# Sums of weight blocks and of X on VectorE, X's sums queued behind the sets, raw weight pieces in three DMAs

## The chip, the core and the metric

The kernel runs on one core of a Trainium2 chip. The metric is the device time of one launch in microseconds (us), the median of several runs. A core has five engines that run their own instruction queues side by side: TensorE (PE in the rows, its weight loads PEld), VectorE (DVE), ScalarE (ACT), GpSimd (POOL) and SyncE (SP, which here only issues DMAs). Each queue is in order: an instruction that waits holds all that stand behind it.

## The reference

Three layers follow each other, all in float32, with 4608 tokens (8 batches of 576) and width 512:

```python
p_packed = softmax(p @ k.T / 8) @ v          # 32 packed queries per head
x = softmax(q @ p_packed.T / 8) @ p_packed   # per head, heads side by side: x is 4608 x 512
h = x @ w_in                                 # 512 -> 2048
x = (h * sigmoid(1.702 * h)) @ w_out         # 2048 -> 512
h = maximum(maximum(x @ w1, x @ w2), x @ w3) # 512 -> 768
out = h @ w_out2                             # 768 -> 512
```

## The kernel before

Each float32 product is made of three TensorE matmuls on high and low parts of both operands (`mm3`, L102 to L104), so every operand is first split: ScalarE casts the high part, another engine subtracts it to get the low part.

The program is one list of steps. Each step has a time in the list (`add(t, fn)`), the steps are sorted by it and written out in that order, and a scheduler then sets each engine's queue from the written order and the data. `tc.issue_after(ins)` adds one more rule: what is written inside stands behind `ins` on the same engine. `latest["dve"]` is the newest VectorE instruction of the main work: the low part of g (L503) while the second layer runs, an instruction of a set (L717) while the third layer runs.

The second layer runs in 256 units: `h_unit` makes a tile of h on TensorE (18 matmuls of a unit with its part of the output), ScalarE and VectorE form t and then g (L495, L496, L501, L503), and `out_unit` multiplies g by w_out two units later. While it runs, from about 640 us of the span, the weights of the third layer are made ready in 18 pieces of 128 partitions. `Piece.load` brings the raw bits of a piece by SP (L580, four DMAs, two raw buffers); `Piece.conv` decodes them with five VectorE and two ScalarE instructions (L554 to L563); `Piece.sums` forms a sum over 128x512 (L588) and four sums and differences over 128x128 (L591 to L594); `split_hi` and `split_lo` (L605, L609) split these, and SP writes them to DRAM (`wsa`, `wss`, L598 and L611). 14 pieces stand in the list beside the second layer, four at the start of the third.

The third layer is Strassen's scheme with seven products instead of eight. X is taken in six blocks of 768 tokens. Of each block four quarters B11, B12, B21, B22 are loaded by SP (`load_x`, L655, 384 KB each), four differences T1 to T4 are formed (`sum_x`, L658, 128x768), and seven of the eight are split (`split_x`, L662 on ScalarE and L663 on VectorE). A block then runs nine sets (`Set`, steps p1, p6, p7, p5, p2, p4, p3, each a product of six matmuls over 384 columns), whose results VectorE adds and maximises out of PSUM (L717), and ends with `out2`, the product with w_out2. A set's weights are fetched from `wsa` and `wss` by GpSimd's queue (`load_set`, L628 and L629) two sets ahead. `x_early` and `x_late` are the steps for X: for block 0 the sums run on GpSimd, for the others on VectorE.

Of the kernel before, what the change touches and what calls it, by code (L numbers as in the profile page):

```python
# [13 lines left out]
ALU = mybir.AluOpType  # L14
# [5 lines left out]
P = 128  # L20
# [18 lines left out]
TP_ = [6.0, 8.5, 5.0]  # L39
# [3 lines left out]
def tile_packed_attention_moe(  # L43
# [13 lines left out]
    nc = tc.nc  # L57
# [19 lines left out]
    def f(t):  # L77
        return t.bitcast(F32)
# [373 lines left out]
    latest = {}  # L452
# [88 lines left out]
    wo2, xs, xv, st = {}, {}, {}, {}  # L541
# [28 lines left out]
    class Piece:  # L570
# [3 lines left out]
        def load(self):  # L574
            p_, x = divmod(self.k, 3)
            self.raw = late["r"].tile([P, 2 * TB], I32, tag="raw", bufs=2, name=f"wraw_{self.n}")
            r = self.raw.rearrange("p (a b) -> p a b", a=4)
            for fc, a, o in ((p_, 0, 0), (p_, 1, 1), (p_ + 3, 1, 2), (p_ + 3, 0, 3)):
                c0 = (2 * a + self.kc) * 2 * P
                nc.sync.dma_start(r[:, o], w123[x, fc][:, c0:c0 + 2 * P])  # L580

        def conv(self):
            self.hl = [c_tile(f"wa{y}_{self.n}") for y in range(2)]
            self.v, self.s = conv_late(self.n, self.raw, *self.hl, TB)

        def sums(self):
            v, s, g = self.v, self.s, nc.gpsimd
            g.tensor_tensor(out=v, in0=f(self.hl[0]), in1=f(self.hl[1]), op=ALU.add)  # L588
            v11, v12, v22, v21 = (v[:, y * P:y * P + P] for y in range(4))
            s1, s2, s3, s4 = (s[:, y * P:y * P + P] for y in range(4))  # L590
            g.tensor_tensor(out=s1, in0=v21, in1=v22, op=ALU.add)  # L591
            g.tensor_tensor(out=s3, in0=v11, in1=v21, op=ALU.subtract)
            g.tensor_tensor(out=s2, in0=s1, in1=v11, op=ALU.subtract)
            g.tensor_tensor(out=s4, in0=v12, in1=s2, op=ALU.subtract)  # L594

        def save_a(self):
            for y in range(2):
# [55 lines left out]
    def load_x(j, n, kh, th):  # L653
        c0 = j * BT + th * HT
        nc.sync.dma_start(xv[n], x2d[:, 2 * kh:2 * kh + 2, c0:c0 + HT])  # L655

    def sum_x(eng, o, a, b):
        eng.tensor_tensor(out=xv[o], in0=xv[a], in1=xv[b], op=ALU.subtract)  # L658

    def split_x(n):  # L660
        hi, lo = xs[n][:, 0], xs[n][:, 1]
        nc.scalar.copy(hi, xv[n])  # L662
        nc.vector.tensor_tensor(out=lo, in0=xv[n], in1=f(hi), op=ALU.subtract)  # L663


    def x_early(j, eng):
        return [
            (0, lambda: load_x(j, "B11", 0, 0)),
            (0.1, lambda: load_x(j, "B12", 0, 1)),
            (0.2, lambda: load_x(j, "B22", 1, 1)),  # L670
            (0.3, lambda: load_x(j, "B21", 1, 0)),
            (5.0, lambda: sum_x(eng, "T1", "B12", "B11")),
            (7.0, lambda: sum_x(eng, "T3", "B22", "B12")),
            (9.0, lambda: sum_x(eng, "T2", "B22", "T1")),
        ]

    def x_late(eng):
        return [
            (0, lambda: split_x("B11")),
            (1.0, lambda: sum_x(eng, "T4", "B21", "T2")),  # L680
            (1.1, lambda: split_x("T2")),
            (2.2, lambda: split_x("T3")),
            (3.3, lambda: split_x("T1")),
            (4.4, lambda: split_x("B21")),
            (5.5, lambda: split_x("T4")),
            (6.6, lambda: split_x("B22")),
        ]

    def f_tile(tag, bufs, name, dt=F32):
# [108 lines left out]
    def add(t, fn, *a):  # L798
        plan.append((t, len(plan), fn, a))

    def conv(t, name, src, store, load=6.0, pool=0, step=0.0):
        raws, it = [], []

        def a():
            raws.append(load_raw(name, src))

        def b_():
            it.append(convert(name, raws[0], pool))
            next(it[0])

        def c_():
            next(it[0])

        def d_():
            store(next(it[0]))

        add(t - load, a)
        add(t, b_)
        add(t + step, c_)
        add(t + 2 * step, d_)  # L820
# [13 lines left out]
    def main():  # L834
# [9 lines left out]
        tn = [0.0] * 300  # L844
# [84 lines left out]
        for idx in range(18):  # L929
            pc = Piece(idx // 2, idx % 2)  # L930
            t = TP + idx * TP_[1] if idx < 14 else TB0 - 10 + (idx - 14) * 10.5
            for dt, fn in (
                (-8 if idx > 1 else -TP_[0] + .2, pc.load), (0, pc.conv), (3, pc.sums), (4, pc.save_a),
                (14 if idx < 14 else 8, pc.split_hi), (16.5 if idx < 14 else 9.5, pc.split_lo),
            ):
                add(max(t + dt, last_at + .2), fn)
        for fc in range(NF2):
# [2 lines left out]
            add(t, conv_wo2, fc)  # L940
        add(tn[240] - .1, open_x)
        add(tn[248] - 4, open_raw, 0)
        for dt, fn in x_early(0, nc.gpsimd):
            add(tn[248] - 3.5 + dt * .7, fn)
        for dt, fn in x_late(nc.gpsimd):
            add(tn[250] + 1.5 * dt, fn)
        add(TB0 - .05, open_ff2)
        DS, DO = 7.3, 24.6
        DB = 9 * DS + DO
# [1 line left out]
        for n in range(9 * NBLK):  # L951
            j, r = divmod(n, 9)
# [9 lines left out]
        for j in range(NBLK):  # L962
            t0 = TB0 + j * DB + 9 * DS
            if j < NBLK - 1:
                if j == 0:
                    add(t0 - 14.1, open_x2)
                for dt, fn in x_early(j + 1, nc.vector):
                    add(t0 - 14 + dt, fn)
                for dt, fn in x_late(nc.vector):
                    add(t0 + 1 + dt * 1.6, fn)  # L970
            for tt in range(3):
                add(t0 + tt * DO / 9, out2, j, tt, [0, 3, 1, 4], True, False)
            for tt in range(3):
                add(t0 + DO / 3 + tt * DO / 18, out2, j, tt, [2, 5], False, True)
            for tt in range(3, 6):
                add(t0 + DO * tt / 6, out2, j, tt, [0, 3, 1, 4, 2, 5], True, True)

    if True:
        main()
        for _, _, fn, a in sorted(plan, key=lambda s: s[:2]):  # L980
            fn(*a)
        late["f"].release()
        late["x"].release()
        spp.release()
# [53 lines left out]
```

## Time and profile before

| | us |
|---|---|
| median of 3 runs | 1418.73 (1418.44 to 1420.18) |
| the profiled execution, its own time | 1418.77 |
| its span from first to last instruction | 1416.9 |
| TensorE busy in the span | 1344.9 (95%) |
| VectorE busy | 989.1 (70%) |
| ScalarE busy | 575.2 (41%) |
| GpSimd busy | 322.6 (23%) |

The busy share of VectorE is a mean over stages that differ: in slices of 35 us it lies between 0.5 and 0.9 or more in the first two layers and between 0.2 and 0.7 in the third. So the profile is read here by stretches of the span, and then by what TensorE waits for in each. [...]

### The profile page before, as it was taken

Reading aid. Unit: us, or ns where it says so; the run is one execution under the profiler, and the core shown is the slowest. Engines: PE = TensorE matmul, PEld = TensorE weight load, DVE = VectorE, ACT = ScalarE, POOL = GpSimd, SP = SyncE. Lnnn points to the kernel's source line nnn. Section 1 sums busy time; section 2 is a strip of 40 time slices with the busy share of each in tenths; the row PEclk is TensorE's granted clock in tenths of the full one; section 3 lists DMA queues with packets and bytes.
Section 4 is the critical chain, followed back from the end, with each engine's and each line's share of the span. In section 5 each row is a group of like instructions: output and inputs, shape, how many; then the busy total and the mean of one; then the engine's idle time right before and its main releaser. Section 6 shows DMA issues by size and latency. Waiting matters only on the chain.

```text
span 1416.9 us, 22472 instructions
## 1 busy us (share of the span) xinstructions
PE 1344.9 (95%) x8450; PEld 1278.2 (90%) x8450; DVE 989.1 (70%) x1850; ACT 575.2 (41%) x1212; POOL 322.6 (23%) x436
## 2 busy tenths in 40 slices
PE   5899789999999999999999899699999999999998
PEld 3688789999999989999888899699989999899997
DVE  6799897887666566759899977564646646466362
ACT  3555555664554555545555552131221311213111
POOL 1110244344331035314344222101101001011000
PEclk8999899999999999999999999899999999999999
DMA  8654313561442224125655539765747747476461
GB/s 310 240 189 150 113 55 108 160 198 42 124 127 77 94 66 131 58 75 190 201 173 173 172 126 299 256 227 174 258 161 248 269 160 250 169 259 216 144 205 45
DMA packets 88524, 237.13 MB, mean 167 GB/s; under 512 B 10848, under 2 KB 40032, under 8 KB 81504
## 3 DMA queue, kind: packets, MB, share of 16 engines
q0 software_dynamic: 24640, 132.66, 27.8%
q1 hardware_dynamic: 63776, 103.05, 21.9%
q8 instruction: 66, 1.08, 0.3%
q14 instruction: 42, 0.34, 0.1%
HBM read 191.89 MB, written 43.78 MB: 166 GB/s over the span
## 4 chain that ended last, share of the span: by engine, by line
PE 75%; DVE 16%; DMA 3%; issue 2%; ACT 2%; POOL 1%; SPq 1%; DVEq 0%; ACTq 0%; POOLq 0%
PE p L102 9%; PE p L103 8%; PE p L104 8%; PE acc L102 7%; PE acc L103 7%; PE acc L104 7%; PE accb L103 3%; PE accb L104 3%; PE accb L102 3%; PE h L102 3%; PE h L104 3%; PE h L103 3%; DVE g L503 2%; DVE t L496 2%; DMA xr<-x2d 1%
## 5 line engine op out<-in xcount | busy, mean ns | idle before, releaser
L102 PE MATMUL acc<-g,wo 128*128 128x288 f32 x1024 | 306.3, 302 | 16.2 <-DVE x L523 5.9
L103 PE MATMUL acc<-g,wo 128*128 128x288 f32 x1024 | 303.8, 297 | 7.6 <-DVE g L503 7.5
L104 PE MATMUL acc<-g,wo 128*128 128x288 f32 x1024 | 303.7, 297 | 0.0
L102 PEld LDWEIGHTS acc<-g,wo 128*128 128x128 f32 x1024 | 194.4, 191 | 22.6 <-issue 6.3
L103 PEld LDWEIGHTS acc<-g,wo 128*128 128x128 f32 x1024 | 195.2, 191 | 12.6 <-DVE g L503 10.2
L104 PEld LDWEIGHTS acc<-g,wo 128*128 128x128 f32 x1024 | 195.2, 191 | 0.7 <-issue 0.3
L503 DVE TENSOR_TENSOR g<-t,g 128x288 fp32r<-128x288 f32 x254 | 142.6, 562 | 44.4 <-ACT g L501 41.2
L501 ACT CAST g<-t 128x288 fp32r<-128x288 f32 x256 | 110.8, 433 | 150.9 <-DVE t L496 149.7
L102 PE MATMUL h<-at,pw 128*128 128x288 f32 x512 | 154.8, 303 | 6.0 <-DVE t L496 4.1
L495 ACT ACTIVATE t<-h 128x288 f32<-128x288 f32 x256 | 104.4, 409 | 123.4 <-PE h L104 120.4
L496 DVE SCALAR_TENSOR_TENSOR t<-t,h 128x288 f32<-128x288 f32 x256 | 114.8, 450 | 55.1 <-ACT t L495 52.6
L103 PE MATMUL h<-at,pw 128*128 128x288 f32 x512 | 152.7, 298 | 0.3 <-POOL at L127 0.3
L104 PE MATMUL h<-at,pw 128*128 128x288 f32 x512 | 152.2, 297 | 0.0
L628 POOL DMA_DIRECT2D wa<-wsa x54 | 28.7, 532 | 426.2 <-PE p L104 413.2
L102 PE MATMUL p<-x_T,ws 128*128 128x384 f32 x324 | 109.3, 337 | 11.4 <-DVE m L717 11.4
L103 PE MATMUL p<-x_T,ws 128*128 128x384 f32 x324 | 109.0, 336 | 0.0
L104 PE MATMUL p<-x_T,ws 128*128 128x384 f32 x324 | 108.8, 336 | 0.0
L717 DVE TENSOR_TENSOR u<-s,p 128x384 f32<-128x384 f32 x54 | 29.9, 554 | 112.7 <-PE p L104 112.7
L102 PEld LDWEIGHTS h<-at,pw 128*128 128x128 f32 x512 | 97.0, 190 | 9.6 <-DVE t L496 6.5
L103 PEld LDWEIGHTS h<-at,pw 128*128 128x128 f32 x512 | 97.1, 190 | 0.7 <-POOL at L127 0.5
L104 PEld LDWEIGHTS h<-at,pw 128*128 128x128 f32 x512 | 97.2, 190 | 0.2
L747 ACT COPY s<-p 128x384 f32<-128x384 f32 x54 | 25.9, 479 | 163.3 <-PE p L104 163.3
(187 smaller groups left out, 3150.6 us busy)
## 6 DMA issues: line engine op xcount, KB each, us to landing
ws<-wss POOLq DMA_DIRECT2D x54, 1024.0 KB, 7.6
wa<-wsa POOLq DMA_DIRECT2D x54, 768.0 KB, 4.6
wi<-wsc POOLq DMA_DIRECT2D x48, 512.0 KB, 4.0
raw_k<-in_k SPq DMA_DIRECT2D x32, 288.0 KB, 3.3
raw_q<-in_q SPq DMA_DIRECT2D x32, 288.0 KB, 2.8
x2d<-x SPq DMA_DIRECT2D x16, 576.0 KB, 3.5
wraw<-in_w SPq DMA_DIRECT2D x72, 128.0 KB, 3.3
wss<-ws SPq DMA_DIRECT2D x36, 256.0 KB, 3.0
```

What stands on the lines that cost most here:

```text
L102: nc.tensor.matmul(o, al, bh, start=start, stop=False, skip_group_check=more)
L103: nc.tensor.matmul(o, ah, bl, start=False, stop=False, skip_group_check=more)
L104: nc.tensor.matmul(o, ah, bh, start=False, stop=stop, skip_group_check=more)
L495: nc.scalar.activation(t, o, AF.Tanh, scale=0.5 * 1.702)
L496: nc.vector.scalar_tensor_tensor(out=t, in0=t, scalar=1.0, in1=o, op0=ALU.add, op1=ALU.mult)
L501: latest["act"] = nc.scalar.copy(g[:, 0], gt[n])
L503: latest["dve"] = eng.tensor_tensor(out=g[:, 1], in0=gt[n], in1=f(g[:, 0]), op=ALU.subtract)
L628: nc.gpsimd.dma_start(a, wsa[n % 9].rearrange("p i h b f -> p (i h b f)"))
L717: latest["dve"] = nc.vector.tensor_tensor(out=o, in0=a, in1=b, op=op)
L747: latest["act"] = nc.scalar.copy(self.s1, self.b1)
```

## The change

`Piece.sums` moves its five instructions from GpSimd to VectorE, behind `latest["dve"]`; the first of them adds the decoded high part before its cast instead of the cast one. `Piece.load` takes three DMAs for the same bytes, one of two quarters and two of one. `sum_x` is always on VectorE and also stands behind `latest["dve"]`. The lists `x_early` and `x_late` become `x_loads` (all four quarters at one time) and `x_steps` (sums and splits mixed), which for blocks 1 to 5 begin in the list 1 us behind t0, the list's time for the end of the nine sets of the block ahead; before, three of the four sums stood 9 to 5 us ahead of t0. The times of the steps of a piece change with that: sums at 4 instead of 3, the split at 6.5 and 9 instead of 14 and 16.5.

```diff
             r = self.raw.rearrange("p (a b) -> p a b", a=4)
-            for fc, a, o in ((p_, 0, 0), (p_, 1, 1), (p_ + 3, 1, 2), (p_ + 3, 0, 3)):
-                c0 = (2 * a + self.kc) * 2 * P
-                nc.sync.dma_start(r[:, o], w123[x, fc][:, c0:c0 + 2 * P])
+            src = [w123[x, y].rearrange("p (a k b) -> p a k b", a=2, k=2)[:, :, self.kc] for y in (p_, p_ + 3)]
+            nc.sync.dma_start(r[:, :2], src[0])
+            for a in range(2):
+                nc.sync.dma_start(r[:, 3 - a], src[1][:, a])
...
         def sums(self):
-            v, s, g = self.v, self.s, nc.gpsimd
-            g.tensor_tensor(out=v, in0=f(self.hl[0]), in1=f(self.hl[1]), op=ALU.add)
+            v, s = self.v, self.s
...
-            g.tensor_tensor(out=s1, in0=v21, in1=v22, op=ALU.add)
-            g.tensor_tensor(out=s3, in0=v11, in1=v21, op=ALU.subtract)
-            g.tensor_tensor(out=s2, in0=s1, in1=v11, op=ALU.subtract)
-            g.tensor_tensor(out=s4, in0=v12, in1=s2, op=ALU.subtract)
+            with tc.issue_after(latest["dve"].ins):
+                nc.vector.tensor_tensor(out=v, in0=v, in1=f(self.hl[1]), op=ALU.add)
+                nc.vector.tensor_tensor(out=s1, in0=v21, in1=v22, op=ALU.add)
+                nc.vector.tensor_tensor(out=s3, in0=v11, in1=v21, op=ALU.subtract)
+                nc.vector.tensor_tensor(out=s2, in0=s1, in1=v11, op=ALU.subtract)
+                nc.vector.tensor_tensor(out=s4, in0=v12, in1=s2, op=ALU.subtract)
...
-    def sum_x(eng, o, a, b):
-        eng.tensor_tensor(out=xv[o], in0=xv[a], in1=xv[b], op=ALU.subtract)
+    def sum_x(o, a, b):
+        with tc.issue_after(latest["dve"].ins):
+            nc.vector.tensor_tensor(out=xv[o], in0=xv[a], in1=xv[b], op=ALU.subtract)
...
+    def x_steps():
         return [
...
+            (0, lambda: sum_x("T1", "B12", "B11")),
+            (0.9, lambda: split_x("B11")),
+            (1.8, lambda: sum_x("T2", "B22", "T1")),
+            (2.7, lambda: sum_x("T4", "B21", "T2")),
+            (3.6, lambda: split_x("T2")),
+            (4.5, lambda: sum_x("T3", "B22", "B12")),
...
-                (-8 if idx > 1 else -TP_[0] + .2, pc.load), (0, pc.conv), (3, pc.sums), (4, pc.save_a),
-                (14 if idx < 14 else 8, pc.split_hi), (16.5 if idx < 14 else 9.5, pc.split_lo),
+                (-8 if idx > 1 else -TP_[0] + .2, pc.load), (0, pc.conv), (4, pc.sums), (5, pc.save_a),
+                (6.5, pc.split_hi), (9, pc.split_lo),
...
-        for dt, fn in x_early(0, nc.gpsimd):
-            add(tn[248] - 3.5 + dt * .7, fn)
-        for dt, fn in x_late(nc.gpsimd):
-            add(tn[250] + 1.5 * dt, fn)
+        add(tn[248] - 3.9, x_loads, 0)
+        for dt, fn in x_steps():
+            add(tn[249] + 2 * dt, fn)
...
-                for dt, fn in x_early(j + 1, nc.vector):
-                    add(t0 - 14 + dt, fn)
-                for dt, fn in x_late(nc.vector):
-                    add(t0 + 1 + dt * 1.6, fn)
+                add(t0 - 14, x_loads, j + 1)
+                for dt, fn in x_steps():
+                    add(t0 + 1 + 1.5 * dt, fn)
```

VectorE's queue in the third layer, before, at the end of set 5 of block 0 (the first number in a name such as t_5 or u3_5 is the set; xr0 to xr5 are the raw X buffers, and L658 forms T1 of block 1):

```order
L717 TENSOR_TENSOR u3_5_10756<-u2_5_10747,p7_5_10749 128x384
L717 TENSOR_TENSOR t_5_3_10765<-u3_5_10756,p5_5_10758 128x384
L658 TENSOR_TENSOR xr4_10890<-xr1_10887,xr0_10886 128x768
L717 TENSOR_TENSOR m_3_3_10627<-t_5_3_10765,m_3_3_10627 128x384
L717 TENSOR_TENSOR m_3_0_10637<-p1_5_10727,m_3_0_10637 128x384
```

The same queue now, at the end of set 8, the last of block 0:

```order
L666 TENSOR_TENSOR x_B22_9750<-xr3_10871,x_B22_9750 128x768
L716 TENSOR_TENSOR g2_8_2_10994<-m_6_2_10841,g2_8_2_10994 128x384
L716 TENSOR_TENSOR g2_8_1_11006<-m_6_1_10849,g2_8_1_11006 128x384
L661 TENSOR_TENSOR xr4_10872<-xr1_10869,xr0_10868 128x768
L661 TENSOR_TENSOR xr5_10873<-xr3_10871,xr4_10872 128x768
L661 TENSOR_TENSOR xr1_10869<-xr3_10871,xr1_10869 128x768
L661 TENSOR_TENSOR xr0_10868<-xr2_10870,xr5_10873 128x768
L666 TENSOR_TENSOR x_T2_9752<-xr5_10873,x_T2_9752 128x768
```

T1 of block 1 moved from the middle of set 5 to behind the last instruction of set 8.

VectorE's queue beside the second layer, now, at the first piece (t_181, g_181 and so on are of the units; wa1_0_0 is the low part of piece 0_0, c0 and c1 its work tiles); before, the five sums were not in this queue:

```order
L563 SCALAR_TENSOR_TENSOR wa1_0_0_7653<-c1_0_0_7655,wraw_0_0_7588 128x512
L503 TENSOR_TENSOR g_181_7686<-t_181_7671,g_181_7686 128x288
L592 TENSOR_TENSOR c0_0_0_7654<-c0_0_0_7654,wa1_0_0_7653 128x512
L496 SCALAR_TENSOR_TENSOR t_182_7700<-t_182_7700,h_182_7693 128x288
L593 TENSOR_TENSOR c1_0_0_7655<-c0_0_0_7654 128x128
L594 TENSOR_TENSOR c1_0_0_7655<-c0_0_0_7654 128x128
L131 TENSOR_TENSOR pw_7_1_7373<-pw_3_3_1_7703,pw_7_1_7373 64x512
L595 TENSOR_TENSOR c1_0_0_7655<-c1_0_0_7655,c0_0_0_7654 128x128
L503 TENSOR_TENSOR g_182_7730<-t_182_7700,g_182_7730 128x288
L596 TENSOR_TENSOR c1_0_0_7655<-c0_0_0_7654,c1_0_0_7655 128x128
```

The five sums (L592 to L596) now lie between the units' t and g, over about one and a half units.

The same queue now, at the last units of the second layer, where X of block 0 is made ready:

```order
L666 TENSOR_TENSOR x_T2_9752<-xr_2_9945,x_T2_9752 128x768
L496 SCALAR_TENSOR_TENSOR t_252_10104<-t_252_10104,h_252_10097 128x288
L503 TENSOR_TENSOR g_252_10123<-t_252_10104,g_252_10123 128x288
L661 TENSOR_TENSOR xr_0_9943<-xr_1_9944,xr_0_9943 128x768
L496 SCALAR_TENSOR_TENSOR t_253_10134<-t_253_10134,h_253_10127 128x288
L523 SCALAR_TENSOR_TENSOR x2_227_9412<-acc_248_0_10046,x2_227_9412 128x288
L523 SCALAR_TENSOR_TENSOR x2_227_9412<-acc_248_1_10050,x2_227_9412 128x288
L666 TENSOR_TENSOR x_T3_9753<-xr_0_9943,x_T3_9753 128x768
L523 SCALAR_TENSOR_TENSOR x2_227_9412<-acc_248_2_10054,x2_227_9412 128x288
```

The four sums and all seven splits of block 0 now stand from g_248 on; before, the four sums were in GpSimd's queue, the first split stood at t_236 and the last between g_250 and t_251.

## Rows read from the trace of the kernel before

**Rows 1.** Stretches of the span: length, busy of PE, PEld, DVE, ACT, POOL; clock, DMA.
```profile
core 0: us, PE busy (x) PEld busy (x) DVE busy (x) ACT busy (x) POOL busy (x), PEclk, DMA share, GB/s
640.00:800.00 160.00, 150.92 (x1078) 144.57 (x1078) 148.23 (x283) 89.81 (x202) 58.41 (x78) 1.00 0.58 192
...
810.77:816.64 5.87, 5.87 (x25) 5.87 (x26) 4.37 (x11) 2.44 (x6) 0.00 (x0) 0.50 0.30 89
...
839.00:859.00 20.00, 20.00 (x153) 20.00 (x152) 13.32 (x30) 8.24 (x18) 1.58 (x3) 1.00 0.43 135
870.00:890.00 20.00, 20.00 (x116) 19.53 (x115) 18.80 (x38) 6.80 (x13) 7.38 (x11) 1.00 1.02 333
903.85:915.24 11.39, 0.00 (x1) 0.00 (x1) 1.95 (x4) 0.49 (x2) 0.00 (x0) 0.71 0.83 312
915.24:919.14 3.90, 3.90 (x13) 3.90 (x13) 3.90 (x8) 1.38 (x4) 0.00 (x0) 0.52 0.00 0
950.00:1400.00 450.00, 450.00 (x2430) 428.85 (x2429) 249.59 (x449) 97.90 (x178) 44.52 (x84) 1.00 0.58 200
```

**Rows 2.** Waits of PE from 800 us on: who, for whom, total us, times, longest.
```profile
PE p L102 <- DVE m L717: 11.4, 1, 11.4
PE acc L102 <- ACT g L501: 5.6, 1, 5.6
```

**Rows 3.** Instructions in order of time at the longer wait: start, us, engine, idle before.
```profile
913.29 0.96 DVE L658 TENSOR_TENSOR xr<-xr,xr 128x768 f32<-128x768 f32 x1 [13.01 <-DMA xr<-x2d]
...
915.24 0.69 PE L102 MATMUL p<-x_T,ws 128*128 128x384 f32 x1 [11.39 <-DVE m L717]
```

**Rows 4.** The same view ahead of the shorter wait.
```profile
804.75 2.56 DVE L663 TENSOR_TENSOR x_B<-xr,x_B 128x768 fp32r<-128x768 f32 x1
...
807.45 1.90 POOL L658 TENSOR_TENSOR xr<-xr,xr 128x768 f32<-128x768 f32 x1 [0.95 <-POOL xr L658]
807.60 2.29 DVE L563 SCALAR_TENSOR_TENSOR wo<-c_o,wraw_o 128x512 fp32r<-128x512 f32 x1
```

**Rows 5.** DVE groups by shape, 640 to 812 us: count, busy us, mean ns.
```profile
L503 DVE TENSOR_TENSOR g<-t,g 128x288 fp32r<-128x288 f32 x61 | 32.8, 537 | 3.6 <-ACT g L501 3.6
...
L558 DVE SCALAR_TENSOR_TENSOR c<-wraw,c 128x512 int32<-128x512 int32 x14 | 11.7, 839 | 0.2 <-ACT c L555 0.2
L557 DVE SCALAR_TENSOR_TENSOR c<-wraw,c 128x512 f32<-128x512 uint16 x14 | 11.4, 814 | 0.1
...
L554 DVE TENSOR_SCALAR c<-wraw 128x512 int32<-128x512 int32 x14 | 9.3, 664 | 4.7 <-DMA wraw<-in_w 4.7
L562 DVE TENSOR_SCALAR wraw<-c 128x512 int32<-128x512 int32 x14 | 9.1, 651 | 0.0
L556 DVE TENSOR_SCALAR c<-wraw 128x512 int32<-128x512 int32 x14 | 8.9, 636 | 0.0
```

**Rows 6.** DVE groups by shape, 779 to 800 us.
```profile
L503 DVE TENSOR_TENSOR g<-t,g 128x288 fp32r<-128x288 f32 x9 | 4.0, 448 | 0.0
...
L558 DVE SCALAR_TENSOR_TENSOR c_o<-wraw_o,c_o 128x512 int32<-128x512 int32 x4 | 2.7, 680 | 0.0
L556 DVE TENSOR_SCALAR c_o<-wraw_o 128x512 int32<-128x512 int32 x4 | 1.7, 418 | 0.0
...
L609 DVE TENSOR_TENSOR ws<-c,ws 128x512 fp32r<-128x512 f32 x2 | 1.4, 678 | 0.0
```

**Rows 7.** POOL and DVE in order of time at one piece's sums.
```profile
680.17 1.32 POOL L588 TENSOR_TENSOR c<-wa,wa 128x512 f32<-128x512 f32 x1 [5.69 <-DVE wa L563]
...
680.31 1.47 DVE L562 TENSOR_SCALAR wraw<-c 128x512 int32<-128x512 int32 x1
```

**Rows 8.** Weights of sets 7 and 8, the transfers: start of issues, and time to landing.
```profile
L629 POOL DMA_DIRECT2D ws<-wss x2: 528/532/537, 895.9 to 903.2; - x2
...
DMA to landing us min/median/max: 10.1/10.9/11.8
```

**Rows 9.** ScalarE's copies out of PSUM after the product p1 of set 8.
```profile
931.87 0.48 ACT L747 COPY s<-p 128x384 f32<-128x384 f32 x1 [8.87 <-PE p L104]
```

More of the change, by code (lines that the diff above doesn't have):

```diff
@@ L663, in split_x, with x_loads @@
         nc.vector.tensor_tensor(out=lo, in0=xv[n], in1=f(hi), op=ALU.subtract)
-    def x_early(j, eng):
+    def x_loads(j):
+        for n, kh, th in (("B11", 0, 0), ("B12", 0, 1), ("B22", 1, 1), ("B21", 1, 0)):
+            load_x(j, n, kh, th)
+    def x_steps():
         return [
[L668 to L686, printed above, removed]
+            (0, lambda: sum_x("T1", "B12", "B11")),
[4 more added lines that the diff above has]
+            (4.5, lambda: sum_x("T3", "B22", "B12")),
+            (5.4, lambda: split_x("T3")),
+            (6.3, lambda: split_x("T1")),
+            (7.2, lambda: split_x("B21")),
+            (8.1, lambda: split_x("T4")),
+            (9.0, lambda: split_x("B22")),
         ]
```

## The prediction

> **What bounds the kernel now.** I read the stretches of the span first [rows 1]. From 950 to 1400 us TensorE is busy for all of 450.00 us at a granted clock of 1.00, and VectorE for 249.59: five of the six blocks of the third layer are bound by TensorE, and nothing on VectorE, GpSimd or SP can shorten them. What can be gained lies ahead of that, where TensorE waits. Of the waits from 800 us on two count, 11.4 and 5.6 us [rows 2]. Between 640 and 800 us TensorE has 150.92 us of work, so it stands for 9.1 us in many short waits, beside a VectorE that is busy for 148.23 of 160 [rows 1].
>
> The longer wait: VectorE sits idle for 13.01 us at 900 to 913 us, in front of an L658, the first sum of X for block 1, until X's load lands [rows 3]. In the middle of block 0's sets this holds the L717 instructions that stand behind it in the queue; they empty the PSUM banks, and TensorE starts again only at 915.24, behind one of them [rows 2, 3]. The load was late, but nobody needed it yet: it was the place in the queue that cost time. [...]
>
> The shorter wait: four sums of X for block 0 run on GpSimd, and beside one of them two VectorE instructions take 2.56 and 2.29 us [rows 4]; the size of the first takes 0.96 [rows 3], that of the second 0.68 [rows 6]. The low part of g comes late, and TensorE waits 5.6 us [rows 2]; then its clock is 0.50 for 5.87 us [rows 1].
>
> **Part 1, X's sums of block 1 behind the sets.** In the new queue L661 stands behind the last g of set 8. The set instructions no longer wait for a transfer; the first instructions that need X are the splits behind set 8's first result. p1 of set 8 ended at 931.87 [rows 9], which without the wait and its clock is 931.87 - 11.39 - 1.87 = 918.6. X landed at 913.29 [rows 3], so it is there with 5.3 us to spare. Gain: 11.39, and 3.90 x (1 - 0.52) = 1.87 for the clock, together 13.3 us. What is late next: the sums and four splits now come behind g_8, eight instructions of 0.96 us, overlapping a little; 7.7 us under the product with w_out2, which has 24.6 us in the list of steps. In blocks 1 to 5 the same move gains and costs nothing, TensorE being full there [rows 1].
>
> **Part 2, X's sums of block 0 on VectorE.** With no tensor instruction on GpSimd there, the slowed instructions return to their own length: 1.60 for the first and 1.61 for the second of [rows 4] alone, and the wait goes with them. Gain: 5.58, and 5.87 x (1 - 0.50) = 2.94 for the clock, together 8.5 us.
> Its price falls between 839 and 859 us, where nine of the eleven X instructions now stand, and the first five sums of weights behind them. VectorE is busy for 13.32 of 20 us there [rows 1], of which two are splits of X already. Each X instruction takes 0.87 to the next (0.96 less the overlap), so 13.3 - 1.7 + 9 x 0.87 + 1.5 = 20.9 us of work for 20. It is the last stretch with a queue of units in front of TensorE. The excess is 0.9; the splits also wait for ScalarE's cast in a full queue. I take 2 us, between 0 (the units run two ahead) and 5 (0.5 for each of the nine).
>
> **Part 3, sums of weights on VectorE, 14 pieces between 640 and 800 us.** Added: five instructions a piece. The one of 128x512 takes 0.68 [rows 6]. None of 128x128 stands alone in these rows; from 0.448 for 288 columns and 0.678 for 512 [rows 6] one column takes 1.03 ns and 128 take 0.28, of which some 0.08 overlap the next where it need not wait. So 0.60 + 4 x 0.20 to 0.28 = 1.4 to 1.7, and I take 1.5: 14 x 1.5 = 21.0 us. From above, with the row of 288 columns for each, it is 0.68 + 4 x 0.45 = 2.5.
> [...]
> Removed: the slowing of VectorE beside GpSimd's sums. The first sum of a piece runs 1.32 us on GpSimd, and an L562 that starts 0.14 us behind it takes 1.47 [rows 7] instead of 0.42 (the same kind and size as L556 in [rows 6]). By groups, against the same forms between 779 and 800 us when GpSimd is idle [rows 5, 6]: L503 61 x (0.537 - 0.448) = 5.4; L558 14 x (0.839 - 0.680) = 2.2; L557, of L558's size, 14 x (0.814 - 0.680) = 1.9; L554, L562 and L556 14 x (0.664 + 0.651 + 0.636 - 3 x 0.418) = 9.8. Together 19.3 us. The balance is 1.7 us more work on VectorE, in a stretch in which its lateness is TensorE's: +1.7.
> The three DMAs: SP has 18 issues fewer and does not bound anything. VectorE waits for raw pieces for 4.7 us before [rows 5]. In the new queue a store of the piece before stands between the first DMA and the two others, but the VectorE instruction it waits for comes right behind the one that frees the buffer. I take 0, from -4.7 to +2. So this part lies between -5 and +7.
>
> **Part 4, four pieces beside the first sets.** Two of them fall where VectorE is busy for 18.80 of 20 us [rows 1], 870 to 890 us: 2 x 1.5 us more, part of it into what lies behind. TensorE does not wait there now [rows 2]. I take 0.5, from 0 to 1.5.
>
> **Sum.** -13.3 - 8.5 + 2.0 + 1.7 + 0.5 = -17.6 us. The profiled execution took 1418.77 us, 1.9 more than its span of 1416.9 and equal to the median 1418.73 within 0.1. So 1401.2. With all low ends -26.8 (1392), with all high ends -8.3 (1410.5).
>
> **Rivals.**
> A, slower: VectorE's slow instructions have another cause than GpSimd's sums. Then part 2's 8.5 and the 19.3 don't come back, and the sums are pure addition: 1418.8 - 13.3 + 21.0 + 2.0 + 0.5 = 1429. It decides from the point where less than 0.37 of the slowing goes (23.5 - 13.3 = 10.2 to make up, out of 19.3 + 8.5). Against it: the instruction of [rows 7] ends with GpSimd's, and the same forms are short in the stretch without it [rows 6]. [...] 0.05.
> B, the sums cost 2.5 us a piece (in a chain, each waiting for the one ahead): 14 x 1.0 more, and 2 in parts 2 and 4: 1417. For it: s2 and s4 do depend on the sums just ahead. Against it: the units' instructions lie between them in the queue, and an instruction of 128 columns is not as long as one of 288. 0.08.
> C, block 0 becomes bound by transfers: with TensorE 13.3 us earlier, the weights of set 8, issued at 903.2 and landed up to 11.8 us later [rows 8], at 915.0, are wanted at 918.6. While TensorE stood, DMA moved at 312 GB/s [rows 1]. If they take half as long again, 920.9, TensorE waits 2.3 us and has some 2 us of low clock: 1405.5. 0.10.
> D, the change doesn't move the wait: VectorE still meets X too early. It would have to land after 918.6, and the queue order says it is asked for only there: the 13.3 us stay, 1414.5. 0.02.
> E, more is gained: with no instruction of 1.3 us or more in VectorE's queue, and the raw pieces in time, most of the 9.1 us of short waits go: 7 us less, 1394. For it: such an instruction holds the g behind it. Against it: VectorE's load is the same. 0.09.
>
> **Chances and range.** My forecast has 0.66, within 1393 to 1409 but for some 0.04. C and nearly all of E lie in the same range, so it holds 0.8: 1393 to 1409. A change within 0.2% (2.8 us), about what a measurement of this kernel can't tell from none, is 1416 to 1421.6. Faster: 0.66 + 0.10 + 0.09 + 0.02 + half of B = 0.91; the rest of B is the same or a little slower, 0.03 and 0.01; slower with A 0.06.
>
> **What would show it.** Part 1: no wait of 10 us on any L717, no L661 with idle time ahead of it that TensorE shares, a clock of 1.00 from 860 to 1400. Part 2: no VectorE instruction of 128x768 above 1.0 us; the stretch of X for block 0 shows VectorE full, and a g or a split of X as what TensorE waits for. Part 3: L503 at 0.45 us in the mean, L554, L556 and L562 at 0.42; L592 at 0.68 and L593 to L596 at 0.28; TensorE's short waits between 640 and 800 us together 9 to 13 us. Rival B shows L593 to L596 one behind the other with idle time, A shows the means of [rows 5] unchanged, C a first matmul of set 7 or 8 that waits for ws or wa, D an L666 with a wait for xr that TensorE shares. The forecast is wrong if VectorE's added 21 us are not matched by the shortening of the others, or if a new wait of more than 5 us stands between 835 and 945 us.

## The result, and the profile after

The changed kernel took 1386.37 us in the median (1385.44 to 1388.66), beside 1419.45 for the kernel before in the same series: a ratio of 0.9767, 95% interval 0.975 to 0.9784. That is 33 us less, where 17.6 were forecast; it lies below the range of 1393 to 1409. The profiled executions are 30.0 us apart in span (1416.9 and 1386.9).

The stretches of the changed kernel, with the columns of [rows 1]:

```profile
640.00:800.00 160.00, 158.85 (x1168) 156.01 (x1167) 156.52 (x374) 97.75 (x216) 5.12 (x8) 1.00 0.61 198
800.00:835.00 35.00, 35.00 (x267) 34.98 (x267) 28.55 (x64) 17.19 (x38) 1.08 (x2) 1.00 0.37 121
835.00:860.00 25.00, 25.00 (x160) 24.91 (x159) 21.83 (x48) 8.77 (x17) 4.23 (x8) 1.00 0.85 291
860.00:930.00 70.00, 70.00 (x376) 66.25 (x375) 50.60 (x98) 20.43 (x36) 7.42 (x14) 1.00 0.86 304
823.00:843.00 20.00, 20.00 (x152) 19.90 (x151) 19.25 (x38) 10.46 (x21) 1.06 (x2) 1.00 0.16 49
```

The last line is the stretch of X's eleven instructions for block 0, which start between 823.24 and 841.68 us.

From 640 to 930 us TensorE stands for 1.15 us in all, and its clock is 1.00 throughout. All its waits from 640 us to the end (who, for whom, total, times, longest), where [rows 2] had 11.4 and 5.6:

```profile
PE acc L102 <- DVE x L529: 0.9, 1, 0.9
PE acc L102 <- ACT x L527: 0.2, 1, 0.2
```

VectorE's groups between 640 and 800 us, which answer to [rows 5] (count, busy us, mean ns, idle time ahead):

```profile
L503 DVE TENSOR_TENSOR g<-t,g 128x288 fp32r<-128x288 f32 x62 | 28.6, 462 | 0.2 <-ACT g L501 0.2
...
L557 DVE SCALAR_TENSOR_TENSOR c<-wraw,c 128x512 f32<-128x512 uint16 x14 | 9.6, 685 | 0.0
L558 DVE SCALAR_TENSOR_TENSOR c<-wraw,c 128x512 int32<-128x512 int32 x14 | 9.6, 685 | 0.0
...
L592 DVE TENSOR_TENSOR c<-c,wa 128x512 f32<-128x512 f32 x14 | 9.6, 682 | 0.0
L562 DVE TENSOR_SCALAR wraw<-c 128x512 int32<-128x512 int32 x14 | 5.9, 422 | 0.0
L554 DVE TENSOR_SCALAR c<-wraw 128x512 int32<-128x512 int32 x14 | 5.9, 421 | 0.8 <-DMA wraw<-in_w 0.7
L556 DVE TENSOR_SCALAR c<-wraw 128x512 int32<-128x512 int32 x14 | 5.9, 420 | 0.0
...
L593 DVE TENSOR_TENSOR c<-c 128x128 f32<-128x128 f32 x14 | 4.0, 283 | 0.0
```

The means are near those that the prediction named: 462 for L503, 421 and 422 for L554 and L562, 682 and 283 for the sums. But VectorE is now busy for 156.52 of 160 us instead of 148.23 (more units fall into the 160 us: 62 of L503 instead of 58), and TensorE waits less, not more. That is the surprise to be explained.

The X steps: the four sums of block 1 now run behind the last g of set 8, with no idle time ahead of them (start, us; groups of rows of one kind are drawn together as x2 or x4):

```profile
911.82 1.02 DVE L716 TENSOR_TENSOR g<-m,g 128x384 fp32r<-128x384 f32 x2
912.76 3.68 DVE L661 TENSOR_TENSOR xr<-xr,xr 128x768 f32<-128x768 f32 x4
916.36 3.56 DVE L666 TENSOR_TENSOR x_T<-xr,x_T 128x768 fp32r<-128x768 f32 x4
```

**Where the time went.** The low parts of g (L503) count the units: the last L503 belongs to unit 255, and counting back from it gives the same unit in each trace. In the trace before, unit 167 has its L503 at 612.45, unit 235 at 800.13, unit 239 at 817.56 and unit 251 at 846.76; in the trace after these are 616.73, 792.42, 801.45 and 830.34.

| stretch | before | after | difference | forecast |
|---|---|---|---|---|
| unit 167 to 235: pieces beside the second layer (part 3) | 187.7 | 175.7 | -12.0 | +1.7 |
| 235 to 239: X's sums of block 0 (part 2) | 17.4 | 9.0 | -8.4 | -8.5 |
| 239 to 251: X's splits of block 0 (price of part 2) | 29.2 | 28.9 | -0.3 | +2.0 |
| 251 to the end: sets of block 0, X of block 1 (parts 1 and 4) | 570.1 | 556.6 | -13.6 | -12.8 |
| sum | | | -34.3 | -17.6 |

Ahead of unit 167, where no instruction of the change stands, the trace after is 4.3 us later. It loses them in its first 46 us, where the mean granted clock is 0.74 beside 0.85 before. In the twelve profiled executions unit 167 lies between 612.0 and 616.7, so the kernels below are compared from there on, beside their medians. Parts 1 and 2 came as forecast. What failed is part 3.

### The profile page after: what moved, and what is told of

Its sections match the earlier page's. It is cut to its first block, busy times and chain, and to the rows that moved or that the text cites. A ratio compares the mean times of both kernels' runs of the same rounds, so it can differ in the third digit from the quotient of the medians.

```text
span 1386.9 us, 22440 instructions
## 1 busy us (share of the span) xinstructions
PE 1340.6 (97%) x8450; PEld 1276.1 (92%) x8450; DVE 989.9 (71%) x1944; ACT 577.3 (42%) x1212; POOL 248.3 (18%) x342
## 4 chain that ended last, share of the span: by engine, by line
PE 88%; DVE 8%; ACT 1%; issue 1%; DMA 0%; SPq 0%; POOL 0%; ACTq 0%; POOLq 0%; DVEq 0%
PE p L102 9%; PE p L104 9%; PE p L103 9%; PE acc L102 9%; PE acc L103 9%; PE acc L104 9%; PE h L102 4%; PE h L104 4%; PE h L103 4%; PE accb L103 4%; PE accb L104 4%; PE accb L102 4%; PE pw L102 1%; PE pw L104 1%; PE pw L103 1%
## 5 line engine op out<-in xcount | busy, mean ns | idle before, releaser
L102 PEld LDWEIGHTS acc<-g,wo 128*128 128x128 f32 x1024 | 193.1, 190 | 14.2 <-issue 6.3
L503 DVE TENSOR_TENSOR g<-t,g 128x288 fp32r<-128x288 f32 x254 | 137.6, 543 | 40.1 <-ACT g L501 36.8
L496 DVE SCALAR_TENSOR_TENSOR t<-t,h 128x288 f32<-128x288 f32 x256 | 114.7, 449 | 52.4 <-ACT t L495 50.2
```

Source lines behind the costliest of these rows:

```text
L102: nc.tensor.matmul(o, al, bh, start=start, stop=False, skip_group_check=more)
L496: nc.vector.scalar_tensor_tensor(out=t, in0=t, scalar=1.0, in1=o, op0=ALU.add, op1=ALU.mult)
L503: latest["dve"] = eng.tensor_tensor(out=g[:, 1], in0=gt[n], in1=f(g[:, 0]), op=ALU.subtract)
```

## The experiments

One table first, since most kernels are read by the same numbers: the time from unit 167 to unit 235, and in it VectorE's busy time (the union of its instructions' rows) and idle time. The last column is the busy time without the rows on c_o and wraw_o, the conversion of w_out2 that follows the pieces. The stretch holds 33 of these instructions before, 28 after, 36 in no_sums and 26 in more_load, so only this column compares the work of the pieces and the units.

| kernel | median us | ratio to before (95%) | unit 167 to 235 | VectorE busy | idle | busy without w_out2 |
|---|---|---|---|---|---|---|
| before | 1419.45 | | 187.7 | 164.5 | 23.2 | 149.1 |
| after | 1386.37 | 0.9767 (0.975 to 0.9784) | 175.7 | 161.1 | 14.6 | 149.2 |
| x_only | 1399.16 | 0.9871 (0.9854 to 0.9889) | 187.4 | 163.5 | 23.9 | 148.2 |
| pool_sums | 1400.0 | 0.9878 (0.986 to 0.9896) | 186.9 | 162.5 | 24.4 | 147.1 |
| old_times | 1385.95 | 0.9784 (0.9764 to 0.9804) | 175.7 | 161.1 | 14.6 | 149.4 |
| four_dma | 1385.41 | 0.9772 (0.9756 to 0.9788) | 175.0 | 161.1 | 13.9 | 149.4 |
| gp_probe | 1414.48 | 0.9965 (0.9952 to 0.9979) | 195.0 | 180.7 | 14.4 | 167.1 |
| more_load | 1406.61 | 0.9904 (0.9889 to 0.9919) | 185.5 | 171.3 | 14.2 | 160.7 |
| no_sums | 1392.28 | 0.9807 (0.9789 to 0.9825) | 178.6 | 148.4 | 30.2 | 133.0 |
| pool_sums_noraw | 1413.75 | 0.9958 (0.9946 to 0.9971) | 200.2 | 163.0 | 37.2 | 147.6 |
| no_sums_noraw | 1387.84 | 0.9779 (0.9766 to 0.9792) | 176.8 | 147.9 | 28.9 | 132.6 |
| after_noraw | 1385.13 | 0.9761 (0.9748 to 0.9774) | 174.7 | 161.0 | 13.7 | 149.4 |

The expectations of the three runs without raw loads name 189.6, 178.3 and 181.2 us for this stretch; those counts hold one unit too many, and the table has the stretches of the same units.

The theories at the start: the gain of part 3 comes from the engine of the sums (GpSimd), from the new times of a piece's steps (order), or from the three DMAs.

### x_only: X's part alone

The kernel before with X's part of the change: `sum_x`, `x_loads`, `x_steps` and the places where they are added.

```diff
-    def sum_x(eng, o, a, b):
-        eng.tensor_tensor(out=xv[o], in0=xv[a], in1=xv[b], op=ALU.subtract)
+    def sum_x(o, a, b):
+        with tc.issue_after(latest["dve"].ins):
+            nc.vector.tensor_tensor(out=xv[o], in0=xv[a], in1=xv[b], op=ALU.subtract)
```

> The kernel before with only X's part of the change: all sums of X on VectorE behind the newest set or g instruction, the new list of X's steps; weight sums stay on GpSimd, four DMAs a piece, old times. By every theory parts 1 and 2 come in full: 13.3 + 8.5 = 21.8 us, so 1397.6 from 1419.4. If the price of 2.0 that I put on X's stretch is real, 1399.6. In its trace the short waits of TensorE between 640 and 800 us stay at about 9 us, since nothing of the weights is changed.

Measured: 1399.16, and by the profiles 19.9 us less from unit 167 to the end. Units 235 to 239 take 9.3 us (8.1 less), 251 to the end 558.8 (11.3 less). Of the missing 2 of part 1, 1.2 are a new wait for the weights of a set; the rest isn't taken apart:

```profile
PE acc L103 <- DVE g L503: 2.7, 5, 1.0
...
PE p L102 <- DMA ws<-wss: 1.2, 1, 1.2
```

So parts 1 and 2 are confirmed apart from part 3, the price of 2.0 isn't there (units 239 to 251 take 29.0 us, 29.2 before), and about 13 us of the median are left for the weights.

### pool_sums, old_times, four_dma: one part of the weights' change undone each

pool_sums is the changed kernel with `Piece.sums` (first piece of the diff) and the times of a piece's steps (second piece) as before; old_times has the second piece alone; four_dma has the loop of four DMAs of the kernel before in `Piece.load`, and nothing else.

```diff
-            with tc.issue_after(latest["dve"].ins):
-                nc.vector.tensor_tensor(out=v, in0=v, in1=f(self.hl[1]), op=ALU.add)
+            g.tensor_tensor(out=v, in0=f(self.hl[0]), in1=f(self.hl[1]), op=ALU.add)
...
-                (-8 if idx > 1 else -TP_[0] + .2, pc.load), (0, pc.conv), (4, pc.sums), (5, pc.save_a),
-                (6.5, pc.split_hi), (9, pc.split_lo),
+                (-8 if idx > 1 else -TP_[0] + .2, pc.load), (0, pc.conv), (3, pc.sums), (4, pc.save_a),
+                (14 if idx < 14 else 8, pc.split_hi), (16.5 if idx < 14 else 9.5, pc.split_lo),
```

> The changed kernel with the weight sums back on GpSimd, at the old times of a piece's steps; X's part and the three DMAs stay. Theory GpSimd (its sums hold single VectorE instructions for 1.3 us or more, and that, not VectorE's total, is what TensorE's short waits come from): the short waits between 640 and 800 us come back to 7 to 9 us, 1394 to 1397.5, and VectorE's busy time there falls back to about 148 of 160. Theory order (the new times of a piece's steps are what counts): the same time, and the next kernel tells. Theory DMA (three DMAs bring the raw pieces in time): 1386 to 1389, short waits 1 to 3 us.

> The changed kernel with the old times of a piece's steps (sums 3, split 14 and 16.5 behind the piece's start, instead of 4, 6.5 and 9); sums on VectorE, three DMAs. Theory GpSimd and theory DMA: no change, 1386.4 within 1. Theory order: the short waits of 640 to 800 us come back, 1393 to 1397.

> The changed kernel with the raw pieces in four DMAs again. Theory GpSimd and theory order: no change, 1386.4 within 1, VectorE waits for raw pieces 0.7 us or a little more. Theory DMA: VectorE's wait for raw pieces goes back to about 4.7 us and TensorE's short waits rise by as much, 1390 to 1394.

Measured: what counts is `Piece.sums`. pool_sums and old_times differ in nothing else, that is, in the engine of the sums, their place in its queue and one operand of the first. They are 14.05 us apart in the median and 11.2 from unit 167 to 235. The old times and the four DMAs, each by itself, change nothing that can be told from the spread. Theories order and DMA fall. The wait for raw pieces is 0.1 us with four DMAs (four_dma) and 4.8 with three (pool_sums): it doesn't go by the DMAs either. VectorE's groups of pool_sums, 640 to 795 us:

```profile
L503 DVE TENSOR_TENSOR g<-t,g 128x288 fp32r<-128x288 f32 x56 | 30.1, 539 | 4.3 <-ACT g L501 4.3
...
L562 DVE TENSOR_SCALAR wraw<-c 128x512 int32<-128x512 int32 x14 | 9.2, 654 | 0.0
...
L554 DVE TENSOR_SCALAR c<-wraw 128x512 int32<-128x512 int32 x14 | 7.3, 524 | 5.1 <-DMA wraw<-in_w 4.8 <-issue 0.3
```

The slowed means are back, and so is VectorE's idle time, ahead of g and of the raw pieces.

### gp_probe and more_load: GpSimd's activity and VectorE's own work, each added

Each adds instructions behind the five sums of a piece on VectorE: gp_probe the first piece of the diff, more_load the second.

```diff
+            nc.gpsimd.tensor_tensor(out=v, in0=f(self.hl[0]), in1=f(self.hl[1]), op=ALU.add)
+            for y in range(4):
+                nc.gpsimd.tensor_tensor(out=scratch, in0=v[:, :P], in1=v[:, P:2 * P], op=ALU.add)
...
+                for _ in range(4):
+                    nc.vector.tensor_tensor(out=s3, in0=v11, in1=v21, op=ALU.subtract)
```

> The changed kernel, and beside each piece's sums on VectorE five GpSimd instructions of the size that the sums had there (one of 128x512, four of 128x128), whose results nobody uses; VectorE's own instructions are those of the changed kernel. Theory slowing (an active GpSimd instruction lengthens VectorE's own): VectorE's instructions become longer by 14 to 19 us in all between 640 and 800 us, on a VectorE with 3.5 us left, so TensorE loses 10 to 16 us: 1396 to 1402, L503 back at about 540 ns and instructions of 1.3 us or more again. Theory dependence (what cost time before was that ScalarE's casts and VectorE's splits waited for GpSimd's results): 1386.4 within 1.5.

> The changed kernel with four more VectorE instructions of 128x128 a piece (the third sum written four times more, the same result): 18 x 4 in all, 56 of them beside the second layer, 0.20 us from one to the next, so 11.5 us more VectorE work there and no GpSimd in it. Theory total (TensorE pays for VectorE's work beyond the 3.5 us that are left): 8 us, 1394, and TensorE's short waits at about 8 us. Theory single hold (only single long instructions make TensorE wait, the total doesn't): 1386 to 1389, short waits under 3 us.

gp_probe: VectorE has the instructions of the changed kernel and needs 180.7 us for them instead of 161.1; the stretch is longer by about as much, 19.3 us, and from 640 to 800 us none of VectorE's waits is for GpSimd. That is over the 16 that theory slowing gave at most, and theory dependence falls. Its groups, 640 to 795 us, the first that reads two operands from SBUF and the next that reads one of them from PSUM:

```profile
L504 DVE TENSOR_TENSOR g<-t,g 128x288 fp32r<-128x288 f32 x52 | 27.8, 536 | 0.0
L497 DVE SCALAR_TENSOR_TENSOR t<-t,h 128x288 f32<-128x288 f32 x53 | 23.6, 445 | 0.6 <-ACT t L496 0.2
...
L559 DVE SCALAR_TENSOR_TENSOR c<-wraw,c 128x512 int32<-128x512 int32 x14 | 12.4, 888 | 0.0
...
L557 DVE TENSOR_SCALAR c<-wraw 128x512 int32<-128x512 int32 x14 | 9.2, 657 | 0.0
```

more_load: 10.2 us more busy time on VectorE, and 9.8 us more from unit 167 to 235, near the 8 of theory total; single hold falls. So the changed kernel is just at the point from which VectorE's work is paid by TensorE. The other 10 us that more_load lost stand elsewhere, and no theory had them. The m of an early set waits, by its row, for a store of `wss`, one that SP issues late; TensorE waits 7.71 us for it (SP, VectorE and TensorE in order of time):

```profile
855.19 15.78 SPq L615 DMA_DIRECT2D wss<-ws  x2
...
866.15 0.56 DVE L718 TENSOR_TENSOR m<-u,p 128x384 f32<-128x384 f32 x1 [10.23 <-DMA wss<-ws]
...
866.76 0.69 PE L102 MATMUL p<-x_B,ws 128*128 128x384 f32 x1 [7.71 <-DVE m L718]
```

In gp_probe the same wait is 9.5 us on VectorE and 5.5 on TensorE. The changed kernel doesn't have it, but isn't far from it: with 0.8 us more a piece it was there.

### no_sums: the sums left out

The changed kernel with `Piece.sums` empty.

```diff
         def sums(self):
+            pass
```

> The changed kernel without the five sums of a piece; the weights of the sums are then not those of the reference, so the output differs from it. By every theory VectorE has 20 us less to do between 640 and 800 us. If TensorE's stretch is already full in the changed kernel, 1385.5 to 1386.5, so the sums cost nothing on VectorE and 14 us on GpSimd; if VectorE's added work still costs, 1382 to 1385.

Measured: neither. Without the sums the kernel isn't as fast as with them on VectorE but slower: 1392.28, and 178.6 us for the stretch instead of 175.7. VectorE has 16.2 us less to do there for pieces and units (133.0 for 149.2), of which 3.5 are filled by more of w_out2's conversion, and stands idle for twice as long, 30.2. It waits for ScalarE, and for raw pieces (640 to 800 us):

```profile
DVE g L503 <- ACT g L501: 6.8, 17, 0.5
DVE t L496 <- ACT t L495: 5.3, 12, 1.0
DVE c L554 <- DMA wraw<-in_w: 5.1, 6, 1.5
```

I take the first two to be harmless, since VectorE is ahead there. The third isn't: L554 stands in the queue in front of the units' t and g, and holds them until the piece has landed. A raw load is issued when the last step (L563) of the piece two ahead is done; with less work between, VectorE comes to the next L554 too early.

### pool_sums_noraw, no_sums_noraw, after_noraw: no raw loads

The same edit in pool_sums, in no_sums and in the changed kernel leaves out the raw loads of pieces 2 to 13.

```diff
         def load(self):
+            y = 2 * self.k + self.kc
+            if 1 < y < 14:
+                self.raw = late["raw", y % 2]
+                return
```

> The kernel pool_sums (weight sums on GpSimd) with the raw loads of pieces 2 to 13 left out; these pieces decode what the first two left in the two buffers, so the weights are not those of the reference. VectorE can't wait for raw pieces any more; it waited 4.8 us for them. From unit 167 to unit 235 pool_sums took 189.6 us, the changed kernel 178.3. Theory slowing alone: about 189, 1399 to 1400. Theory both (the slowing, and raw pieces that come late): 184 to 186, 1395 to 1397. Theory raw alone: 178 to 180, 1388 to 1390.

> The kernel no_sums with the raw loads of pieces 2 to 13 left out in the same way. VectorE waited 5.1 us for raw pieces in no_sums, and the stretch from unit 167 to 235 took 181.2 us, longer than with the sums on VectorE (178.3). If the late raw pieces hold up the units behind them in VectorE's queue, the stretch falls to 176 to 178 and the time by 3 to 5 us, to 1387 to 1389. If they don't, it stays at 181 and 1392.

> The changed kernel with the raw loads of pieces 2 to 13 left out in the same way: the control. VectorE waited 0.7 us for raw pieces there, so by every theory no change: the stretch 178 within 1, 1386.4 within 1.5. If it falls by more, the loads cost something by their traffic or on SP's queue and the two kernels beside it are to be read against this one.

no_sums_noraw: 4.4 us faster in the median (1387.84), as expected; from unit 167 to 235 it is only 1.8 (176.8 for 178.6), where I gave 3 to 5. The control is 1.2 us faster in the median and 1.0 in the stretch. So raw pieces that come late cost a us or two of the stretch where VectorE is ahead of them. pool_sums_noraw is a miss by all three theories: 13.3 us more in the stretch, 1413.75. Without the wait for raw pieces VectorE runs into the next one, on GpSimd itself (640 to 930 us):

```profile
DVE c L556 <- POOL c L600: 12.3, 10, 1.3
```

L556 writes a work tile c that GpSimd's sums of the piece ahead still use. In pool_sums this wait does not appear; by my reading the late raw piece had already held VectorE there until the sums were done. How much of the 11.2 us between pool_sums and old_times is slowed instructions and how much held tiles can't be told from this run, since taking one wait away changed the order of all; what the runs show is that both hang on the sums being GpSimd's.

## Why the prediction was wrong, point by point

**Part 1** (-13.3) was right. From unit 251 to the end the changed kernel is 13.6 us faster, and the wait of [rows 3] is gone, and with it the clock of 0.52 behind it [rows 1]: it is 1.00 from 860 to 930 us.

**Part 2** (-8.5) was right: 8.4. Its price was mis-sized, 2.0 forecast and none found. From 823 to 843 us, where X's instructions stand, VectorE is busy for 19.25 of 20 us, nearly full, where 20.9 were reckoned, and TensorE for all of them; the lower bound, 0, was the one that held.

**Part 3** is the step that failed, and not by its terms. Added work: 21.0 forecast; the 70 instructions of the sums take 20.2 us in the changed kernel from the start of each to the start of the next, 1.44 a piece (0.61 and four times 0.21). Relief: 19.3 forecast; with the means of the changed kernel for the same groups (462, 685, 685, 421, 422, 420) it is 18.2. The balance, +1.7 forecast, is +0.1 by VectorE's busy time without w_out2 (149.1 to 149.2). So VectorE has as much to do as it had, nearly as forecast, and yet the stretch is 12.0 us shorter, outside the -5 to +7 that I gave.

What failed is the sentence behind the balance, that the stretch is one "in which its lateness is TensorE's", so that TensorE pays for each us of it and gets back each us. The rows of before spoke against it: VectorE was busy for 148.23 of 160 us [rows 1], so it was idle for 11.8, while TensorE stood for 9.1 beside it. An engine that is idle for longer than the other waits isn't bound by the sum of its work. I read it as late in bursts, behind a slowed instruction or a wait at the head of its queue, and idle between; that picture is taken from the waits, and no run tests it alone. The runs put it so: taking GpSimd's sums away gives TensorE 8.3 us (186.9 to 178.6), until TensorE's own work is nearly all that is left, 174.54 of the 175.7 us in the changed kernel. The sums on VectorE then go into time in which it would have been idle (30.2 us, then 14.6) and cost TensorE nothing; it gains 2.9 more, of which no_sums_noraw puts 1.8 down to raw pieces that VectorE no longer runs ahead of. Only from there on is a us on VectorE about a us on TensorE: more_load paid 9.8 for 10.2, gp_probe 19.3 for 19.6.

The 9.1 us were also too few. TensorE's waits before, from 640 to 800 us:

```profile
PE acc L103 <- DVE g L503: 2.7, 6, 0.7
PE pw L102 <- issue: 1.8, 1, 1.8
PE acc L102 <- ACT x L527: 1.8, 2, 1.6
PE acc L102 <- DVE x L529: 1.5, 3, 1.0
PE h L102 <- DVE t L496: 1.0, 2, 0.6
```

These are only the pauses that outlast a matmul's row. Where TensorE does not wait, a row is 0.29 us long, and the next starts 0.13 behind its start:

```profile
783.00 0.29 PE L103 MATMUL h<-at,pw 128*128 128x288 f32 x1
783.13 0.30 PE L104 MATMUL h<-at,pw 128*128 128x288 f32 x1
783.26 0.29 PE L102 MATMUL h<-at,pw 128*128 128x288 f32 x1
```

So about 0.16 us of each pause does not show. From the first matmul of h_167 to the first of h_235 both traces have the same 1275 matmuls, in 187.1 us before and 174.9 after. At the median distance of each kind before (0.13, and 0.235 for the 39 on pw) they would take 172.7 us, an estimate; so TensorE lost 14.4 us before and loses 2.2 now.

Which engine was behind can be read from ScalarE's waits, a view that I didn't use. Before, 640 to 795 us:

```profile
ACT g L501 <- DVE t L496: 47.8, 44, 2.8
...
ACT t L495 <- PE h L104: 4.0, 7, 1.1
```

and after:

```profile
ACT g L501 <- DVE t L496: 25.5, 33, 1.5
ACT t L495 <- PE h L104: 21.0, 26, 2.6
```

Before, ScalarE waited for VectorE's t, up to 2.8 us at a time, and hardly ever for TensorE's h, which lay there already. After, it waits for TensorE nearly as much as for VectorE's t: TensorE is often the last of the three now.

**The DMAs of part 3**: 0 was right for the edit (four_dma), but I had put the 4.7 us of waiting for raw pieces [rows 5] down to the loads, as something that only the DMAs could change. They went to 0.7 because VectorE comes to a piece later in its queue; without the sums it comes early, and waits 5.1 us (no_sums).

**Part 4** (+0.5): nothing; TensorE is full from 860 to 930. But more_load shows a step there, not a slope: one late store costs TensorE 7.7 us at once.

**The rivals.** A fell: pool_sums and gp_probe show GpSimd as the cause. B fell: the small sums take 283 ns with 0.20 from one to the next (862.10, 862.30, 862.50 for three in a row), the third of which reads what the first wrote. C showed in x_only, pool_sums, old_times, no_sums, pool_sums_noraw and no_sums_noraw as waits of 1.1 to 1.6 us for ws, not in the changed kernel. D fell. E came, in full and more: 7.9 of the 9.1 us of short waits, and the stretch 12.0 shorter. It had 0.09. The argument against it, "VectorE's load is the same", was true and didn't bear on it. With E in full and no prices my own terms give 13.3 + 8.5 + 7.9 = 29.7 us. That this is near the 30.0 of the spans is luck: the stretches give 34.3, less the 4.3 by which the changed kernel's profiled execution, its slowest (1388.66), was late at unit 167; the medians give 33.1. What the terms lack is the part of TensorE's pauses that its rows hide.

## What to carry to other kernels

Before work is added to an engine and relief set against it, compare its idle time with the time that the other engine waits for it: where both stand in the same stretch, as here, the load isn't the bound, the bursts are, and what removes single long instructions or waits at the head of a queue can be worth more than the balance (here 12.0 us, at a balance of +0.1). Count TensorE's loss from the starts of the same matmuls and not from its busy share, which hides the short pauses (14.4 us here, 9.1 by the share). Count units and pieces on both sides: a stretch of the span holds other work after a change than before it. The waits of the engine in the middle tell which of its two neighbours is behind. Such a stretch has a floor, the other engine's own work, and here a slope of about one beyond it: take off the interference first, fill the idle time to that point, and no further.

## What the runs showed of the hardware

GpSimd's instructions lengthened some of VectorE's here and left others alone. With GpSimd's sums (pool_sums) and without (after), L503, which reads two operands from SBUF, takes 539 and 462 ns in the mean, L554 524 and 421, L562 654 and 422. L496, which reads one operand from PSUM, takes 446 and 448, and L131, out of PSUM too, 685 and 685. GpSimd's were lengthened too: its 128x512 add, 1.32 us in [rows 7], took 3.26 at one place of gp_probe, in the middle of a row of VectorE instructions:

```profile
698.96 3.26 POOL L598 TENSOR_TENSOR c<-wa,wa 128x512 f32<-128x512 f32 x1 [1.89 <-DVE c L597]
702.29 3.26 POOL L600 TENSOR_TENSOR scratch<-c 128x128 bf16<-128x128 f32 x4
```

L554 and L562 read a single operand, from SBUF, and were lengthened as well, so two operands in SBUF are not needed for it. By what the two engines hold each other up, no run here shows. The price, as measured: five GpSimd instructions a piece lengthened VectorE's busy time in gp_probe by 19.6 us for 14 pieces, 1.4 a piece, as much as doing the sums on VectorE takes (1.44).
